# Moving the value products and the turning within the early steps of a fused attention and squared-ReLU kernel

## Chip, core and metric

The kernel runs on one core of a Trainium2 chip. The metric is the device time of one execution in microseconds (us). The profile is one more execution of the same program, recorded by the hardware profiler. Engines are named as in it: PE (TensorE), PEld (its weight loads), DVE (VectorE), ACT (ScalarE), POOL (GpSimd) and SP (SyncE). L387 is line 387 of the kernel before.

## What is computed

Attention with a threshold, followed by two matrix products with a squared ReLU between them, all in fp32:

```
scores = q @ k^T / 8                          # 8 batches x 8 heads, 576 x 576, head size 64
keep   = scores >= max(scores) - tau
w      = where(keep, exp(scores - max(scores)), 0);  w = w / sum(w)
x      = (w @ v), the 8 heads side by side    # 4608 tokens x 512
out    = (max(x @ w_in, 0) ** 2) @ w_out      # 512 -> 2048 -> 512
```

## The kernel before

**Steps.** The attention goes through pairs of heads ("visits"), and through each visit in blocks of 128 query rows, four whole ones and a short one of 64 rows (block 4), in which both heads are put side by side in one operand (`qmid`). One block of one visit is a step. The first eight steps are blocks 0 and 1 of four head pairs, the next twelve blocks 2, 3 and 4 of the same pairs, so that the first 256 tokens of x are complete early; then come whole visits of five steps. Up to step 34 the weights are turned by PE ("turned" means transposed, so that the keys lie on partitions). From step 35 on DVE and DMA turn them, in a different routine.

**What a step does.** Step s works on three blocks at once:

- its own block: scores on PE (L273, L266 for the short block) into PSUM banks 0 to 3, maxima on DVE (L310), three small ACT instructions and the exponentials on ACT (`exponents`, L322, L323, L325), threshold and sum on DVE (L337 to L340), division on POOL (L345, L347, `divide`). The next step's scores of a head write where the threshold of this step reads, so they follow it;
- the block of step s-2: its weights are turned, `turn(vis, i, part)`. Each of three parts is three transposes on PE (L386) into one PSUM bank and a copy on ACT into `wT` (L387). The short block has eight narrow transposes in two parts (L393, L395) and two in the third (L399, L400);
- the block of step s-3: its values, `mix`. Ten matmuls with v (L502, twenty records in the trace) go into one PSUM bank, and ACT copies the result into the token buffer `xT` (`put`, L485).

Values and turning take their banks in turn from 4 and 5 (`take("tx", (4, 5))`). Only in the first ten steps, while `early()` holds, the turning's second part takes from 6 and 7 instead. A matmul into a bank waits until the copy that empties the bank has run.

**Other work in the same steps.** Each step can round one or two pieces of the second stage's weights (`round_weights`, stages 0 to 4): two ACT instructions (L149, L150), two on DVE (L152, L154), two on POOL (L156, L158). The first piece's ACT part is issued at the very start of a step, ahead of the scores, and a second piece's behind the exponentials. Three buffers serve in turn, so a rounding waits for the POOL part of the third last piece. Once 256 tokens of x are complete, `add_chunk` puts the matmuls of the second stage in a list, 16 pieces of `x @ w_in` (L548, followed by ACT's L558 and POOL's square L559) and then pieces with `w_out` (L730). `fill` takes pieces out of the list to put them between the attention's PE work, as `rate` spreads them over the steps to come.

**Order.** The program is issued by hand, in the order of the code; each engine has one queue in that order. In the main loop of a step the lines that matter here are 1106 to 1202: round_weights stage 0, scores and maxima, turning parts 0 and 1 (L1127), exponents (L1131), a second piece's rounding, the qmid copies (`split_left`, L242, in the second step of a visit), the first fill, values with `add_chunk` (L1149), turning part 2 (L1153), threshold and the other rounding stages, the other fills, and last the end of the rounding. `mixes` says at which step which values are made, `chunk_at` at which step a chunk of 256 tokens is complete.

Of the kernel before, what the change touches and what calls it, by code (L numbers as in the profile page):

```python
# [19 lines left out]
def kernel(  # L20
# [177 lines left out]
    def some_loads():  # L198
        for _ in range(min(1 + (len(loads) > 8), len(loads))):
            to, src = loads.popleft()  # L200
            nc.sync.dma_start(out=to, in_=src)
# [117 lines left out]
    def exponents(vis, i):  # L319
        w, sc, st = weights[vis, i]  # L320
        mx, thr, bias = (st[:, j, 0:len(sc)] for j in range(3))
        nc.scalar.activation(out=bias, in_=mx, func=AF.Copy, scale=-SCALE)  # L322
        nc.scalar.activation(out=thr, in_=mx, func=AF.Identity, bias=ntau8)  # L323
        for u in range(len(sc)):
            nc.scalar.activation(out=w[:, u, :].rearrange("p (h k) -> p h k", h=2), in_=sc[u],  # L325
                                 func=AF.Exp, bias=bias[:, u:u + 1], scale=SCALE)
# [27 lines left out]
    def take(what, among):  # L354
        used[what] += 1
        return bank[among[used[what] % len(among)]]
# [21 lines left out]
    def turn(vis, i, part):  # L378

        w = weights[vis, i][0]  # L380
        ps = take("mm", (6, 7)) if early() and part == 1 else take("tx", (4, 5))
        ps = ps.rearrange("p (c n) -> p c n", n=P)
        if i < NBLK:
            for n in range(3):
                c = 3 * part + n
                nc.tensor.transpose(ps[:, n, :], w.rearrange("p u k -> p (u k)")[:, c * P:(c + 1) * P], ident)  # L386
            nc.scalar.copy(wT[:, 2 * i:2 * i + 2, 3 * part:3 * part + 3, :].rearrange("p g c q -> p c g q"),  # L387
                           ps[:, 0:3, :].rearrange("p c (g q) -> p c g q", g=2))
        elif part < 2:
            rows = slice(part * D, (part + 1) * D)  # L390
            for c in range(NBLK):
                at = part * REST + c * P
                nc.tensor.transpose(ps[:, c, 0:D], w[rows, 0, at:at + P], ident[rows, rows])  # L393
            at = part * (NBLK + 1)
            nc.scalar.copy(wT[:, 2 * NBLK, at:at + NBLK, :], ps[:, :, 0:D])  # L395
        else:

            for rows, keys in ((slice(0, D), slice(S - REST, S)), (slice(D, P), slice(0, REST))):
                nc.tensor.matmul(ps[rows, 0, 0:D], w[rows, 0, keys], ident[rows, rows], start=True, stop=True)  # L399
            nc.scalar.copy(wT[:, 2 * NBLK, NBLK, :], ps[:, 0, 0:D])  # L400
# [98 lines left out]
    def mix(n, cols):  # L499

        def term(ps, u, c, at, rows=slice(0, P), first=False, last=False):
            nc.tensor.matmul(ps[u * D:(u + 1) * D, :], vs[n % 2][rows, u * (NBLK + 1) + c, :],  # L502
                             wT[rows, at // REST:(at + ps.shape[1]) // REST, NBLK if c == NBLK else u * (NBLK + 1) + c, :],
                             start=first, stop=last)

        above, below = slice(0, D), slice(D, P)
        arrived(vs[n % 2])
        if not by_dma(n):
            ps = take("tx", (4, 5))[:, 0:cols.stop - cols.start]
            for c in range(NBLK + 1):  # L510
                for u in range(2):
                    term(ps, u, c, cols.start, first=(c == 0), last=(c == NBLK))
            put(n, cols.start, ps, False)
            return
        n1, n2 = 2 * P + REST, 2 * P
        at = ODD if paired(n) and n % 2 else ONE
        one, two = bank[0], bank[4]
        groups = (one[:, 0:n1], at, (above, below)), (two[:, 0:n2], TWO, (below, above))
        for ps, x, _ in groups:
            for c in range(NBLK):  # L520
                for u in range(2):
                    term(ps, u, c, x, first=(c == 0))

        for ps, x, places in groups:
            for u, rows in enumerate(places):
                term(ps, u, NBLK, x, rows, last=True)
        put(n, 0, one[:, ONE - at:ONE - at + 2 * P], True)
        left = ODD if at == ODD else LEFT - at
        put(n, NBLK * P, one[:, left:left + REST], False)
        put(n, 2 * P, two[:, 0:n2], True)  # L530
# [303 lines left out]
    mixes = {}  # L834
# [16 lines left out]
    chunk_at, j = {}, 0  # L851
# [11 lines left out]
    def early():  # L863
        return state["step"] < min(chunk_at)
# [16 lines left out]
    def add_chunk(j):  # L881
        waiting.extend(pieces_of(j))
        whole.add(j)
# [212 lines left out]
    for s in range(END + 1):  # L1096
        state["step"] = s
        if s >= first_late:
            assert 4 not in kept.values()
            late_step(s)  # L1100
            continue
        state["usable"] = rounded_by[-1]
        rounded_by.append(state["rounded"])
        on = s < NST
        now = []
        if on:
            n, i = steps[s]
            at = visits[n][1].index(i)
            last = at == len(visits[n][1]) - 1
            now = list(range(done, done + pieces[s]))  # L1110
            done += pieces[s]
            more = n + 1 < len(visits)
            short = n < 2 * HP
            if short and at == 0 and 0 < n + 1 < 2 * HP:
                load_qk(n + 2)
            elif not short and at == 1 and not by_dma(n):
                load_qk(n + 1)
            if now:
                round_weights(now[0], 0)
            if s != 1:  # L1120
                scores(s)
                after()
                some_later("gpsimd")
        old = steps[s - 2] if 2 <= s < NST + 2 and not by_dma(steps[s - 2][0]) else None
        at_once = now or old or early()
        lay = on and last and more and not by_dma(n) and s != 1
        if old:  # L1127
            turn(*old, 0)
            turn(*old, 1)
        if on:  # L1130
            exponents(n, i)  # L1131
            if s and by_dma(steps[s - 1][0]):
                turn_last(s)
            for p in now[1:]:
                round_weights(p, 0)
            if at == 1:
                split_left(n)
            if lay:
                prep(n + 1)
            elif now:  # L1140
                for p in now:
                    round_weights(p, 1)
        if s in mixes and not old:
            mix(*mixes[s])
            for j in chunk_at.get(s, ()):
                add_chunk(j)
        quarter = rate(s) / 4 if s < END else 1e9
        fill(quarter)
        if s in mixes and old:  # L1149
            mix(*mixes[s])  # L1150
            for j in chunk_at.get(s, ()):
                add_chunk(j)
        if old:  # L1153
            turn(*old, 2)
        state["free"] = s > first_dma
        if s == 0:
            scores(1)
            prep(1)
        smooth = s > first_dma + 2 and s not in mixes
        some_later("vector")  # L1160
        some_later("gpsimd")
        if smooth:
            after()
        if on:
            threshold(n, i)
            for fn in prep_at[s] + load_at[s]:
                fn()
            if lay and now:
                round_weights(now[0], 1)
            if now:  # L1170
                round_weights(now[0], 2)
                round_weights(now[0], 3)
            for p in now[1:]:
                assert not lay
                round_weights(p, 2)
                round_weights(p, 3)
            if not at_once:
                divide(n, i)
        if smooth:
            fill(quarter)  # L1180
            after()
            some_later("gpsimd")
        for what in place_at[s]:
            place_blocks(*what)
        some_loads()
        some_later("vector")
        if not smooth:
            some_later("gpsimd")
            fill(quarter)
        some_loads()  # L1190
        if on and at_once:
            divide(n, i)
        fill(quarter)
        some_loads()
        fill(quarter)
        some_loads()
        if on:
            for p in now:
                end_rounding(p)
            if at == 0 and 0 < n <= 2 * HP:  # L1200
                load_v(n)
            elif last and n >= 2 * HP and not by_dma(n):
                load_v(n + 1)
# [35 lines left out]
```

## Time and profile before

| what | value |
|---|---|
| median of 3 runs | 1334.75 us (1334.66 to 1335.83) |
| the profiled execution's own time | 1334.19 us |
| its span in the profile | 1332.4 us |
| mean granted TensorE clock | 0.995 |
| PE busy | 1297.2 us, 97% of the span |
| PE weight loads busy | 1078.2 us, 81% |
| DVE busy | 928.2 us, 70% |
| POOL busy | 758.3 us, 57% |
| ACT busy | 585.2 us, 44% |
| mean HBM traffic | 133 GB/s |

The busy times are sums over the whole span. Since the engines work on different blocks at the same moment, an engine's share doesn't tell by itself what the end waits for; this is read from the chain of waits (each piece of work that ended last before the next could start) and from the timeline, by stage. The first steps start at 8.50 us (steps 0 and 1), 14.64 (step 2), 21.48 (step 3) and 28.84 (step 4); step 10 starts at 59.68 us, step 20 at 120.43 and step 35 at 210.18.

### The profile page before, as it was taken

What the parts mean: (1) busy time and instruction counts of PE and PEld (TensorE: products, weight loads), DVE (VectorE), ACT (ScalarE), POOL (GpSimd) and SP (SyncE); (2) the same over time, 40 slices, a digit from 0 to 9 for tenths busy, and PEclk for the clock granted to TensorE, in tenths of its full rate; (3) what the DMA queues carried; (4) which work ended last, traced back from release to release, by engine and by line L of the source; (5) the groups of instructions that cost most, each with busy time, mean ns of one, the idle gap of its engine ahead of it and who ended that gap; (6) DMA issues with size and microseconds to landing.
All of it is one profiled execution on the core that took longest, in us unless ns stands there. A gap on an engine that the chain in (4) does not pass through costs nothing.

```text
span 1332.4 us, 25133 instructions
## 1 busy us (share of the span) xinstructions
PE 1297.2 (97%) x9112; PEld 1078.2 (81%) x9112; DVE 928.2 (70%) x2026; ACT 585.2 (44%) x1357; POOL 758.3 (57%) x865
## 2 busy tenths in 40 slices
PE   7898999999999999999999999999999999999998
PEld 5676556878796979787888888888887888889997
DVE  6877776777787878777786777868687877732131
ACT  4776674235262535343434443444434343422321
POOL 4689875765655555364655554737274737354451
PEclk7999999999999999999999999999999999999999
DMA  8764531647767686867586685758677577430000
GB/s 159 160 152 117 144 91 36 160 93 183 167 177 170 169 195 165 200 141 200 123 186 147 172 192 138 189 108 205 138 181 169 150 180 164 141 91 1 17 17 16
DMA packets 330124, 186.68 MB, mean 140 GB/s; under 512 B 291440, under 2 KB 291472, under 8 KB 323600
## 3 DMA queue, kind: packets, MB, share of 16 engines
q1 hardware_dynamic: 317696, 116.87, 45.0%
q10 hardware_dynamic: 9504, 59.27, 11.2%
q0 software_dynamic: 2800, 8.93, 1.8%
q8 instruction: 72, 1.18, 0.4%
q14 instruction: 52, 0.43, 0.1%
HBM read 109.22 MB, written 68.42 MB: 133 GB/s over the span
## 4 chain that ended last, share of the span: by engine, by line
PE 85%; DVE 5%; ACT 4%; DMA 3%; POOL 2%; issue 1%; SPq 1%; ACTq 0%; DVEq 0%; POOLq 0%
PE big L659 28%; PE big L765 27%; PE big L502 10%; PE big L289 8%; PE big L548 3%; PE big L273 3%; PE big L730 2%; PE big L386 2%; DMA wT<-aside 2%; DVE st L310 1%; DVE w L337 1%; ACT w L325 1%; ACT wT L387 1%; DMA aside<-turned 1%; PE big L266 0%
## 5 line engine op out<-in xcount | busy, mean ns | idle before, releaser
L337 DVE SCALAR_TENSOR_TENSOR w<-big,st,w 128x576 f32<-128x576 f32 x269 | 207.2, 807 | 97.8 <-ACT w L325 97.5
L310 DVE TENSOR_REDUCE st<-big 128x1 f32<-128x576 f32 x288 | 204.3, 748 | 86.2 <-PE big L289 53.5
L347 POOL TENSOR_SCALAR w<-w,st 128x576 f32<-128x576 f32 x269 | 247.4, 929 | 28.0 <-DVE st L340 24.0
L765 PE MATMUL big<-wo,gsum 128*128 128x256 f32 x1088 | 243.8, 382 | 0.0
L345 POOL TENSOR_SCALAR st<-st 128x2 f32<-128x2 f32 (+1 forms) x148 | 36.6, 247 | 358.6 <-DVE w L337 354.2
L765 PEld LDWEIGHTS big<-wo,gsum 128*128 128x128 f32 x1088 | 204.4, 190 | 37.1 <-issue 8.6
L659 PE MATMUL big<-xT,w_in_sb 128*128 128x128 f32 x1536 | 187.3, 277 | 0.8 <-DVE g L671 0.7
L659 PEld LDWEIGHTS big<-xT,w_in_sb 128*128 128x128 f32 x1536 | 178.5, 192 | 9.8 <-issue 7.6
L765 PE MATMUL big<-wo,g 128*128 128x256 f32 x816 | 185.3, 382 | 0.1
L325 ACT ACTIVATE w<-big,st 128x576 f32<-128x576 f32 x269 | 183.8, 734 | 0.2 <-ACT st L323 0.2
L502 PE MATMUL big<-wT,vs 128*64 128x128 f32 (+5 forms) x1700 | 164.8, 355 | 9.7 <-ACT wT L387 4.2
L765 PEld LDWEIGHTS big<-wo,g 128*128 128x128 f32 x816 | 151.6, 190 | 26.1 <-issue 6.5
L502 PEld LDWEIGHTS big<-wT,vs 128*64 128x64 f32 (+1 forms) x1700 | 97.3, 137 | 73.9 <-issue 21.5
L322 ACT ACTIVATE st<-st 128x2 f32<-128x2 f32 (+1 forms) x148 | 30.3, 205 | 263.4 <-DVE st L310 262.2
L671 DVE TENSOR_TENSOR g<-big,g 128x512 f32<-128x512 f32 x96 | 64.8, 677 | 82.3 <-PE big L659 76.4
L289 PE MATMUL big<-kT,qT 64*128 64x320 f32 (+3 forms) x768 | 108.0, 416 | 0.2 <-DVE w L337 0.2
L289 PEld LDWEIGHTS big<-kT,qT 64*128 64x128 f32 x768 | 84.5, 186 | 15.7 <-issue 4.3
L538 POOL TENSOR_TENSOR gsum<-g 128x512 f32<-128x512 f32 x34 | 46.1, 1356 | 81.6 <-ACT g L668 72.1
L667 ACT ACTIVATE g<-g 128x512 f32<-128x512 f32 x96 | 60.3, 628 | 61.0 <-DVE g L671 59.4
L668 ACT ACTIVATE g<-g 128x512 f32<-128x512 f32 x128 | 80.7, 630 | 4.1
L431 DVE STREAM_TRANSPOSE turned<-w 128x512 f32<-128x512 f32 x100 | 70.3, 703 | 3.7 <-DMA aside<-turned 2.6
L437 DVE STREAM_TRANSPOSE turned<-w 128x512 f32<-128x512 f32 x100 | 66.9, 669 | 0.0
(113 smaller groups left out, 1973.2 us busy)
## 6 DMA issues: line engine op xcount, KB each, us to landing
aside<-turned ACTq DMA_DIRECT2D x50, 1152.0 KB, 5.2
wT<-aside SPq DMA_DIRECT2D x200, 288.0 KB, 5.5
vs<-in_v_dram SPq DMA_DIRECT2D x72, 128.0 KB, 4.4
ql<-in_q_dram SPq DMA_DIRECT2D x126, 72.0 KB, 2.9
wo<-in_moe_w_in_dram SPq DMA_DIRECT2D x16, 512.0 KB, 4.8
wo<-in_moe_w_out_dram SPq DMA_DIRECT2D x16, 512.0 KB, 3.7
out_dram<-osb POOLq DMA_DIRECT2D x32, 256.0 KB, 3.3
kl<-in_k_dram SPq DMA_DIRECT2D x113, 72.0 KB, 3.0
```

The costliest lines, as they stand in the source:

```text
L289: nc.tensor.matmul(big[to, at + x0:at + x1], lhsT, keys[u * D:(u + 1) * D, x0:x1], start=True, stop=True)
L310: nc.vector.tensor_reduce(out=mx[:, u:u + 1], in_=sc[u], axis=AX.XY, op=ALU.max)
L325: nc.scalar.activation(out=w[:, u, :].rearrange("p (h k) -> p h k", h=2), in_=sc[u], func=AF.Exp, bias=bias[:, u:u + 1], scale=SCALE)
L337: nc.vector.scalar_tensor_tensor(out=wu, in0=sc[u], scalar=thr[:, u:u + 1], in1=wu, op0=ALU.is_ge, op1=ALU.mult, accum_out=sm[:, u:u + 1])
L347: nc.gpsimd.tensor_scalar(out=w[:, u, :], in0=w[:, u, :], scalar1=z[:, u:u + 1], scalar2=rcp[:, u:u + 1], op0=ALU.add, op1=ALU.mult)
L431: move(wb[:, 0:h, :, :], whole_[:, 0, :, :, :])
L437: move(wb[:, h + 1:, :, :], whole_[:, 1, :, :, :])
L502: nc.tensor.matmul(ps[u * D:(u + 1) * D, :], vs[n % 2][rows, u * (NBLK + 1) + c, :], wT[rows, at // REST:(at + ps.shape[1]) // REST, NBLK ...
L659: nc.tensor.matmul(to[:, f, :], factor(j, p, q, c)[:, f * P:(f + 1) * P], part[:, c, :], start=(p in "125" and f == 0 and c == 0), stop=(p ...
L668: nc.scalar.activation(out=to, in_=to, func=AF.Square)
L671: nc.vector.tensor_tensor(out=x, in0=to, in1=x, op=ALU.add)
L765: nc.tensor.matmul(to, left[:, f, :], wo[:, slot, f, :], start=(f == 0), stop=(f == HF - 1))
```

## The change

Only the order of issue in steps 2 to 36 changes; no instruction is added, removed or given another shape. In each step that turns a block,

- the values of the block before are issued right behind the scores, and `add_chunk` with them, so it also runs ahead of `rate` and the first fill;
- the exponentials are issued next, behind the values and their copy, ahead of the turning and of ACT's copies of it;
- turning parts 0 and 1 come behind the exponentials, but ahead of a second rounding piece and of the qmid copies;
- turning part 2 goes to the end of the step, behind the last fill.

```diff
@@ -1125,10 +1125,16 @@
         at_once = now or old or early()
         lay = on and last and more and not by_dma(n) and s != 1
         if old:
+            if s in mixes:
+                mix(*mixes[s])
+                for j in chunk_at.get(s, ()):
+                    add_chunk(j)
+        if on:
+            exponents(n, i)
+        if old:
             turn(*old, 0)
             turn(*old, 1)
         if on:
-            exponents(n, i)
             if s and by_dma(steps[s - 1][0]):
                 turn_last(s)
             for p in now[1:]:
@@ -1146,12 +1152,6 @@
                 add_chunk(j)
         quarter = rate(s) / 4 if s < END else 1e9
         fill(quarter)
-        if s in mixes and old:
-            mix(*mixes[s])
-            for j in chunk_at.get(s, ()):
-                add_chunk(j)
-        if old:
-            turn(*old, 2)
         state["free"] = s > first_dma
         if s == 0:
             scores(1)
@@ -1194,6 +1194,8 @@
         some_loads()
         fill(quarter)
         some_loads()
+        if old:
+            turn(*old, 2)
         if on:
             for p in now:
                 end_rounding(p)
```

## Prediction

> **What bounds the kernel now.** I call one pass of the main loop a step and number it as the code does; it begins where its scores (L273, or L266 for the short block) start. First the windows view, cut where the change ends to act: the three stretches that follow are steps 4 to 9, steps 10 to 35, and most of the rest.
>
> ```profile
> 28.84:59.68 30.84, 26.49 (x223) 19.52 (x223) 24.68 (x60) 22.65 (x58) 17.88 (x24) 1.00 0.79 158
> 59.68:223.81 164.13, 152.49 (x1168) 105.77 (x1168) 118.44 (x262) 113.80 (x280) 130.22 (x141) 1.00 0.46 116
> 223.81:1200.00 976.19, 970.35 (x6798) 818.61 (x6798) 733.66 (x1619) 402.64 (x933) 549.77 (x629) 1.00 0.67 160
> ```
>
> After the stretch come busy times of PE, weight loads, DVE, ACT, POOL. Past 223.81 PE is busy 99% of the time and the change leaves that part's order alone, so what is won or lost before comes out at the end undiminished. Only the first 224 us are open: PE idles 4.4 us in steps 4 to 9 and 11.6 us in steps 10 to 35, where POOL is busy 79%. Next the chain of waits in an early step (7) and in a later one (14):
>
> ```profile
> 43.94 1.97 PE big L273 x7
> 45.91 0.49 PE big L386 x3
> 46.42 0.86 ACT wT L387 x2
> 47.48 0.75 ACT wo L325
> 48.25 0.84 DVE wo L337 x2
> ...
> 82.12 1.17 PE big L273 x8
> 83.29 0.81 PE big L386 x6
> 84.10 1.73 PE big L548 x8
> 85.83 1.24 PE big L502 x20
> 87.07 0.48 PE big L386 x3
> 87.55 1.73 PE big L548 x8
> ```
>
> Step 7 is a ring of 5.19 us: scores, first third of the turning, ScalarE's two copies of it, exponential, threshold, next scores. PE is not its bound. Step 14 is PE alone: 7.16 us with two pieces of the second stage (L548), so 5.43 with one and 3.70 with none. The timeline says why ScalarE is in step 7's ring:
>
> ```profile
> 45.25 1.46 DVE L310 TENSOR_REDUCE st<-big 128x1 f32<-128x576 f32 x2
> 46.42 0.86 ACT L387 COPY wT<-big 128x384 f32<-128x384 f32 x2 [2.23 <-PE big L386]
> 46.64 1.31 PE L502 MATMUL big<-wT,vs 128*64 128x128 f32 x20
> 47.17 0.22 ACT L322 ACTIVATE st<-st 128x2 f32<-128x2 f32 x1
> 48.74 0.27 ACT L485 COPY xT<-big 128x128 f32<-128x128 f32 x1
> ```
>
> The maxima end at 46.71, but L322, which opens the exponentials, waits for the copies until 47.17: 0.46 us. And POOL's hand in step 17:
>
> ```profile
> 101.73 2.66 POOL L158 TENSOR_TENSOR w_in_sb<-turned 128x512 f32<-128x512 f32 x2
> 103.19 0.68 ACT L150 ACTIVATE turned<-wo 128x512 f32<-128x512 uint32 x1 [3.15 <-POOL w_in_sb L158]
> 104.44 0.70 PE L548 MATMUL big<-xT,w_in_sb 128*128 128x256 f32 x2 [0.50 <-POOL w_in_sb L158]
> 104.97 0.23 ACT L322 ACTIVATE st<-st 128x2 f32<-128x2 f32 x1
> ```
>
> ScalarE stands 3.15 us at a rounding (L150) until POOL frees its buffer, and the exponentials queue behind.
>
> [...] Here two banks serve values and turning, and PE waits 0.24 us at L502 for a copy of the turning in steps such as 13 and 25. [...] L152 takes 0.42 us alone, and 1.36 us at 138.79 beside POOL's L158. [...] The trace shows 2.40 us for the values at 25.91 and 1.31 us from 31.05 on.
>
> **The change, early steps.** No instruction is added or removed. On PE the values (1.31) move ahead of the turning; on ScalarE the copy of the values (L485) moves ahead of the exponentials with them, and only the copies of the turning go behind. So in step 7 L322 no longer waits for 0.49 + 0.86 of turning; it waits for 1.31 of values and for L485. PE's scores end at 45.91, values then at 47.22; L485 starts 0.05 later (as in step 29, where values end at 182.53 and it starts at 182.58), and the next instruction starts 0.15 after it (48.74 to 48.89): L322 at about 47.4 in place of 47.17. That is 0.20 a step, as the rest of the ring stays: 5 steps (4 to 8), +1.00. Step 2 has no values, so its exponentials do gain: maxima end 19.03, L322 was at 19.55: -0.47. Step 3 runs on the slow clock, values 2.40, and L322 comes 0.7 later, but PE's own work held its end already: +0.10. Step 9 also copies qmid (L242), which step 10's scores need; it stood right behind the exponentials and now stands behind two copies (0.75): 0.20 + 0.75 = +0.95. Sum +1.58.
>
> **Steps 10 to 36.** In these the maxima (1.42) start only when all scores are there, so values (1.24 on the chain) lie beside them: L322 can start 2.75 us after the step's scores, as before (2.73). What changes is PE. Values used to wait for a copy of the turning to free a bank (0.5 us on the chain where no piece lay between); this goes. The chunk is announced before the first filling, so pieces come earlier: by the two programs' instruction order steps 10 to 13 have 1, 2, 1, 0 pieces (before 0, 1, 2, 1), then 2, 2, 0 repeated (before 2, 1, 1), steps 20 to 27 have 2, 2, 1, 2, 1, 1, 2, 1 (before 2, 1, 2, 1, 2, 1, 1, 2), and the same from 28. A step lasts as long as the longer of PE's sum and the ring. Block changes alter 5.43 and 7.16: narrow values (0.73) save 0.5, the short block's turning (0.5 and 0.26 for 0.80 and 0.48) saves 0.5, its scores 0.2.
> Steps 10 to 13: before 22.37 (59.68 to 82.05). After 5.22 (PE), 7.15 (PE), 5.37 (exponentials, two copies, qmid), 4.25 (threshold behind the transposes of DVE) = 21.99: -0.38.
> Steps 14 to 20: before 46.30 (to 128.35). Step 14 stays 7.15. Step 15 rounds two pieces; its second rounding is issued after the turning, so L149, L152 and the threshold come 0.65 later: exponentials end 4.3 into the step, and 0.65 + 0.58 + 0.5 + 0.82 follow: 6.36 becomes 6.87. Step 16 without a piece gets 4.42 for 5.04, but step 17 gives it back: L485 stands behind L150, which POOL releases 7.6 us after step 16's start, and the second third of the turning needs the bank that L485 empties, with two pieces behind it on PE. 7.6 + 0.6 + 0.3 (L485) + 0.4 (turning) + 3.5 (pieces) + 0.5 = 12.9 for both, before 12.96. Step 18, 6.90 (VectorE's L152 then lies beside no L158: 0.43 for 0.95, which pays for its delay); 19 and 20 like 16 and 17. Sum 7.15 + 6.87 + 12.9 + 6.9 + 12.9 = 46.72: +0.42.
> Steps 21 to 24: before 27.47 (to 155.82). After 6.63 (two pieces, short turning), 7.0 (two roundings; VectorE's L152 beside no L158), 7.13 (two pieces), 5.2 (one piece). The last was 8.51 with two, 1.57 of it PE waiting for copies behind L150 behind POOL; POOL's square (L559) moves out of this stretch's way into an idle 2.6 us. Sum 25.96: -1.51.
> Steps 25 to 29: before 28.84 (to 184.66); after 5.43 + 6.63 + 5.2 + 5.43 + 5.2 = 27.89: -0.95, the removed bank waits.
> Steps 30 to 33 had a piece between turning and values: no change. Step 34: L322 waits for values and L485, +0.32. Step 35: two L736 copies no longer straddle the values, so PE's 1.05 us stall at L548 becomes 0.6: -0.37.
> SP's queue keeps its order; POOL's changes only in five squares. Sum 1.58 - 0.38 + 0.42 - 1.51 - 0.95 + 0.32 - 0.37 = -0.89. The profiled execution took 1334.19 us (span 1332.4 and 1.8 around it), so 1333.3; the median of the runs is 0.56 above it: 1333.8.
>
> **What the trace of before doesn't show.** How long ScalarE's backlog holds L485 in the other steps. Roundings (1.16) begin when the last copy is done and end near 1.6 us into a step, values end near 2.45: from below 0, from above 1.2 us as in step 17, in up to 4 more steps. I take 0. The moment at which the clock rises: from -1.1 (step 3's values at 1.31 for 2.40) to +1.5 (a step more on the slow clock, which lasts 6.84 for 5.19). I take 0.
>
> **Rivals.** Slower: L485 becomes the gate. It holds the exponentials and the second third of the turning together, and any rounding that waits for POOL now holds it. It decides once POOL's L158 ends over 1.8 us into a step's scores. For it: POOL's 79%, and three roundings that waited already (6.3 + 2.6 us). Against: between them ScalarE has 0.8 us to spare. Price: four more steps at 1.2 = +4.8, so 1338.6.
> Faster: POOL's chain starts earlier with step 16's scores, and steps 17 and 20 don't pay back (2 x 1.25)[...]: -0.9 - 2.5 - 1.1 = -4.5, so 1330.3. For it: step 17's wait is 3.15 us of POOL alone; against: between the double roundings of steps 15 and 18 (96.95 to 116.78) POOL idles only 1.4 us of 19.8, so it can't run far ahead.
> That the exponentials don't come ahead at all: for the early steps this is the forecast itself, since L485 stays ahead of them. If L485 cost the early ring only 0.05, the sum would be -1.6: 1333.1, inside the forecast.
>
> **How the numbers follow.** About 0.2% (2.7 us) is what a measurement of this kernel can tell from no change. Forecast, 0.50: 1333.8, alone 1332.1 to 1337.4. Slower rival 0.27, near 1338.6; faster rival 0.23, near 1330.3. The range reaches to both, 1330.3 to 1338.6, and leaves their outer parts out. Faster 0.23, same 0.50, slower 0.27.
>
> **What would show it.** In steps 4 to 8 a ring of 5.4 us, with values and L485 in the chain in place of L386 and L387, and L322 right behind L485. Step 10's scores late, behind L242. In steps 17 and 20 L386 waiting for L485 behind L150. Step 24 some 3 us shorter, steps 21, 23 and 26 over 1 us longer. From 224 us on the same distance to the end. I am wrong if the ring gets shorter than 5.19, if L386 waits for L485 in most steps, or if the part after step 36 changes its length.

## The result and the profile after

| | before | after |
|---|---|---|
| median of 5 runs beside each other | 1335.83 us (1334.66 to 1336.67) | 1341.69 us (1340.59 to 1342.33) |
| profiled execution, its span | 1334.19, 1332.4 us | 1341.71, 1339.9 us |
| granted TensorE clock, profiled execution | 0.995 | 0.991 |
| PE busy | 1297.2 us | 1304.5 us |
| start of scores, steps 4, 10, 21, 25, 36, 38 | 28.84, 59.68, 128.35, 155.82, 223.81, 241.37 | 28.57, 62.68, 131.59, 160.40, 228.14, 246.03 |

The changed kernel takes 1.005 times as long (95%: 1.0038 to 1.0062): slower by 6 us, where 1333.8 us was forecast and 1338.6 us was the end of the range. The windows view of the changed kernel, cut at the same work (steps 4 to 9, steps 10 to 35; after the stretch come PE, weight loads, DVE, ACT, POOL, then the clock):

```profile
28.57:62.68 34.11, 27.70 (x222) 21.45 (x222) 25.97 (x62) 23.14 (x61) 18.61 (x24) 0.95 0.77 163
62.68:228.14 165.46, 156.87 (x1168) 108.44 (x1169) 115.15 (x259) 111.56 (x278) 128.86 (x140) 0.99 0.44 113
```

The first stretch is 34.11 us for 30.84, the second 165.46 for 164.13. PE is busy longer in both (27.70 for 26.49, 156.87 for 152.49), and yet has the same matmuls; the last column but two gives one reason: the clock was 1.00 in both stretches before and is 0.95 and 0.99 now. In each of the two it stood at half for 3.41 us, which by estimate costs 1.7 us at most, half of that time. The first stretch's 1.2 us are within that; the second's 4.4 us are not. A further 2 us of them are, by estimate, five steps in which two groups of transposes take 0.89 us for 0.46 (the experiments on the short block). The chain of waits in steps 7 and 14:

```profile
44.77 1.97 PE big L273 x7
46.75 1.29 PE big L502 x20
48.04 0.02 issue
48.06 0.27 ACT xT L485
48.33 0.10 ACT st L322
...
48.52 0.75 ACT wo L325
...
49.30 0.84 DVE wo L337 x2
...
84.80 1.24 PE big L273 x8
86.04 1.24 PE big L502 x20
87.28 0.94 PE big L386 x6
88.22 3.46 PE big L548 x16
91.68 0.33 PE big L386 x3
```

Step 7 is a ring again, now 5.40 us (5.19 before): values (L502) and their copy (L485) stand where the turning and its copies stood, as the prediction said. Step 14 is PE alone, 7.14 us, as before. The timeline of step 7:

```profile
46.09 1.45 DVE L310 TENSOR_REDUCE st<-big 128x1 f32<-128x576 f32 x2
46.68 1.31 PE L502 MATMUL big<-wT,vs 128*64 128x128 f32 x20
48.06 0.27 ACT L485 COPY xT<-big 128x128 f32<-128x128 f32 x1 [2.44 <-PE big L502]
48.22 0.21 ACT L322 ACTIVATE st<-st 128x2 f32<-128x2 f32 x1
```

The maxima (L310) end at 47.54 and L322 could run. ACT is idle for 2.44 us, but L485 is ahead of it in the queue, and L485 waits until PE has done the values. L322 starts 0.68 us after the maxima; it was 0.46. In step 17 the wait for POOL is still there, shorter, and the second third of the turning waits for L485 behind it, as predicted:

```profile
106.79 0.67 ACT L150 ACTIVATE turned<-wo 128x512 f32<-128x512 uint32 x1 [2.18 <-POOL w_in_sb L158]
107.36 0.25 ACT L485 COPY xT<-big 128x128 f32<-128x128 f32 x1
107.66 0.55 PE L386 MATMUL big<-ident,w 128*128 128x128 f32 x3 [1.11 <-ACT xT L485]
```

What the prediction had not seen is in the windows of PE. The record of the granted clock holds only 1.00 and 0.50 in the profiles of the two kernels. In the changed one half the clock stands from 13.45 to 27.10 us, then three times for 3.41 us, beginning at 57.82, 146.56 and 573.23 us. The view is cut at these edges: three windows, each with the one that follows it (PE busy, then clock, DMA share, GB/s):

```profile
54.40:57.82 3.42, 2.36 (x16) 1.00 0.85 182
57.82:61.23 3.41, 3.41 (x26) 0.50 0.93 264
143.15:146.56 3.41, 1.53 (x8) 1.00 0.18 31
146.56:149.98 3.42, 3.42 (x18) 0.50 0.72 253
569.82:573.23 3.41, 1.28 (x10) 1.00 1.23 182
573.23:576.64 3.41, 3.34 (x16) 0.50 0.51 65
```

Each time a window in which PE is busy for 38 to 69% is followed by one at half the clock. PE's longest single gaps there were 1.06 us ahead of step 9, 1.66 in step 22 and 2.20 at 571 us. The matmuls then take longer: scores 2.98 us for 1.24 in step 23, values 2.12 for 1.31 in step 9 and 4.26 for 2.63 at 573 us. The kernel before has no stretch at half speed between the start, up to 28.5 and 29.1 us in its two profiles, and the end, although PE idles there too:

```profile
148.01:151.42 3.41, 1.84 (x22) 1.00 0.06 11
151.42:154.84 3.42, 3.42 (x21) 1.00 0.81 229
```

So the busy time of a window does not decide alone (1.84 us here without a fall, 2.36 at 54.40 with one); the part on why the prediction was wrong comes back to it. Over the 70 executions of the kernel before in the comparisons below the granted clock is 0.994 to 0.996; over the five of the changed kernel it is 0.989 to 0.994.

### The profile page after: what moved, and what is told of

Its sections match the earlier page's. It is cut to its first block, busy times and chain, and to the rows that moved or that the text cites. A ratio compares the mean times of both kernels' runs of the same rounds, so it can differ in the third digit from the quotient of the medians.

```text
span 1339.9 us, 25103 instructions
## 1 busy us (share of the span) xinstructions
PE 1304.5 (97%) x9112; PEld 1083.1 (81%) x9112; DVE 924.5 (69%) x2026; ACT 582.8 (43%) x1357; POOL 755.8 (56%) x865
## 4 chain that ended last, share of the span: by engine, by line
PE 85%; DVE 5%; DMA 4%; ACT 3%; SPq 1%; POOL 1%; issue 1%; ACTq 0%; DVEq 0%; POOLq 0%
PE big L659 29%; PE big L765 27%; PE big L502 11%; PE big L289 8%; PE big L273 3%; PE big L548 3%; PE big L730 2%; PE big L386 1%; DMA wT<-aside 1%; DVE w L337 1%; DVE st L310 1%; ACT w L325 1%; DMA aside<-turned 1%; DMA vs<-in_v_dram 1%; DVE wo L718 1%
## 5 line engine op out<-in xcount | busy, mean ns | idle before, releaser
L310 DVE TENSOR_REDUCE st<-big 128x1 f32<-128x576 f32 x288 | 204.5, 748 | 90.7 <-PE big L289 54.0
L347 POOL TENSOR_SCALAR w<-w,st 128x576 f32<-128x576 f32 x269 | 247.0, 927 | 28.5 <-DVE st L340 24.2
L502 PE MATMUL big<-wT,vs 128*64 128x128 f32 (+5 forms) x1700 | 167.6, 359 | 4.2 <-DMA wT<-aside 3.3
L502 PEld LDWEIGHTS big<-wT,vs 128*64 128x64 f32 (+1 forms) x1700 | 99.0, 139 | 72.0 <-issue 26.3
L322 ACT ACTIVATE st<-st 128x2 f32<-128x2 f32 (+1 forms) x148 | 30.1, 203 | 263.6 <-DVE st L310 263.1
```

What stands on the lines that cost most here:

```text
L310: nc.vector.tensor_reduce(out=mx[:, u:u + 1], in_=sc[u], axis=AX.XY, op=ALU.max)
L347: nc.gpsimd.tensor_scalar(out=w[:, u, :], in0=w[:, u, :], scalar1=z[:, u:u + 1], scalar2=rcp[:, u:u + 1], op0=ALU.add, op1=ALU.mult)
```

## The experiments

Theory "waits": L485 ahead of the exponentials, and what else the new order makes wait, costs the time. Rival "clock": the waits are small, and the time is lost in half-speed stretches, taken to come from PE's idle time. Step lengths are from one profiled execution each, from the start of one step's scores to the next one's. The start of step 3 moves by up to 1.4 us between executions of one kernel, so sums are also given from there to step 38's scores: 219.89 us before, 225.00 after.

**Exponentials ahead of the values in the early steps.**

```diff
+        if on and early():
+            exponents(n, i)
         if old:
             if s in mixes:
...
-        if on:
+        if on and not early():
             exponents(n, i)
```

> The changed kernel, but in the early steps the exponentials are issued ahead of the values, so that the copy of the values (L485) stands behind them on ScalarE; later steps as in the changed kernel. Theory 'waits' (the early ring is 5.40 us because L485 stands ahead of the exponentials): the ring of steps 4 to 8 falls to about 4.7 us (5.40 less 0.5 for the values and 0.2 for the copy beyond the maxima), seven steps of it give 4 us: about 1337.5 us for 1341.7. Rival 'clock' (the loss is lost TensorE clock after idle gaps, the ring itself costs nothing or little): with PE as the next bound of the ring or with its idle gaps shorter the time moves with the granted clock alone; if the dips at 57.5 and 145.5 us stay, at most 1 us is won.

Measured: 1336.96 us, 1.0008 (0.9999 to 1.0017) of before, so nearly all of the loss is gone. Step 3 to step 38: 220.19 us. But the ring is 5.07 us and not 4.7. The timeline of PE in its step 7 shows L485 once more:

```profile
45.02 0.88 PE L386 MATMUL big<-ident,w 128*128 128x128 f32 x6
46.87 0.55 PE L386 MATMUL big<-ident,w 128*128 128x128 f32 x3 [0.98 <-ACT xT L485]
47.35 0.99 PE L273 MATMUL big<-kT,qT 64*128 64x288 f32 x4
```

L485 now stands behind the exponentials, and the last third of the turning, which uses the bank that L485 empties, waits 0.98 us for it, with the next scores behind. The ring gave 0.33 us a step. About half of the 4.8 us between steps 3 and 38 came from the clock, by estimate from two steps: step 3 left the slow clock of the start earlier (5.90 us for 7.54, 1.6 less), which may be luck, since the next run issues step 3 in the same order and took 7.28; and step 9 stayed on the full one (values 1.31 for 2.12, 0.8 less). So each theory has half of it. The slow stretches at 143 and 569 us stayed.

**The same, and a bank of its own for the last third.**

```diff
-        ps = take("mm", (6, 7)) if early() and part == 1 else take("tx", (4, 5))
+        ps = take("mm", (6, 7)) if early() and part else take("tx", (4, 5))
```

> The run before it (exponentials ahead of the values in the early steps), with the last third of the turning in a bank of its own in the early steps, since there the ring was 5.07 us, with PE waiting 0.84 us for L485, which had gone behind the exponentials, to empty the bank that this third takes. Theory (L485 held that ring too, through the bank): the ring falls to 4.7 us (5.40 less 0.20 for L485 and less 0.49 for a place ahead of the copies), 0.35 less for six steps: step 10 starts 2.1 us sooner than with the exponentials ahead alone. Rival (PE's own sum of some 4.6 us or the threshold holds the ring as well): 5.0 us, under 0.5 us won.

Measured: 1334.95 us, 0.9997 (0.9988 to 1.0006) of before. The ring is 4.67 to 4.88 us in turn, and its timeline shows nothing between turning and scores but the threshold:

```profile
46.39 0.20 ACT L322 ACTIVATE st<-st 128x2 f32<-128x2 f32 x1 [1.79 <-DVE st L310]
46.73 1.20 PE L386 MATMUL big<-ident,w 128*128 128x128 f32 x9
47.93 0.27 ACT L485 COPY xT<-big 128x128 f32<-128x128 f32 x1
48.47 0.75 PE L273 MATMUL big<-kT,qT 64*128 64x288 f32 x2 [0.53 <-DVE wo L337]
```

So L485 held both rings, first through ACT's queue and then through the bank; its rival (PE or the threshold hold the ring at 5.0) falls. The gain of 2.1 us at step 10 did not come in the profiled execution: step 3 took 7.28 us for 5.90, and step 5 had a half-speed stretch (5.89 us), so that step 10 started 0.85 us later than in the run above. The clock takes and gives more than this wait.

**Two thirds of the short block in one bank.**

```diff
-        ps = take("mm", (6, 7)) if early() and part == 1 else take("tx", (4, 5))
-        ps = ps.rearrange("p (c n) -> p c n", n=P)
+        if i < NBLK or part != 1:
+            ps = take("mm", (6, 7)) if early() and part == 1 else take("tx", (4, 5))
+            used["turning"] = ps
+        if i == NBLK:
+            ps = used["turning"][:, part % 2 * 4 * D:(part % 2 + 1) * 4 * D].rearrange("p (c n) -> p c n", n=D)
+        else:
+            ps = ps.rearrange("p (c n) -> p c n", n=P)
```

> The changed kernel, but the two thirds of the short block's turning use two halves of one PSUM bank, so that the second no longer waits for L485 to empty the bank of the values. Theory 'waits': steps 15, 18, 21, 26 and 31 are shorter by 0.36, 0.25, 0.5, 0.5 and 0.5 us, 2.2 in sum: about 1339.5 us. Rival 'clock': TensorE only waits elsewhere (the chain of the threshold holds those steps), under 0.7 us is won: 1341 to 1341.7.

Measured: 1355.5 us, 1.0152 (1.0138 to 1.0166) of before, a miss for both. The steps grew, 15, 18 and 21 to 8.99 us, 26 to 10.58 (with a half-speed stretch in it, one of five in this profile after the start): PE waits 1.82 us for the copy of the first third, which stands behind the exponentials. In step 15 the first four transposes end at 98.48 us, that copy at 100.25, and the second four start at 100.30. The edit put a longer wait for the one it took away, and so did not tell the theories apart.

**Second third of the short block behind half of the pieces; and both thirds there.** The second of these (labelled as the pair) moves part 0 with it.

```diff
             turn(*old, 0)
-            turn(*old, 1)
+            if old[1] < NBLK:
+                turn(*old, 1)
...
         fill(quarter)
+        if old and old[1] == NBLK:
+            turn(*old, 1)
```

> The changed kernel, with the second third of the short block's turning issued behind the first half of the pieces of its step, so that the pieces lie beside PE's wait for L485 to empty the bank. Theory 'waits': steps 15, 18, 21, 26 and 31 fall from 7.23, 7.15, 7.16, 7.16 and 5.44 us to 6.87, 6.9, 6.63, 6.63 and 4.9: 2 us sooner by step 36. Rival (L485 stands behind other work than this shows, or the sum of PE was taken too small): these steps stay within 0.15 us of what they were.

> The changed kernel, with both thirds of the short block's turning (one on array rows 0 to 63, one on 64 to 127) issued together behind the first half of the pieces. In the kernel before the 8 took 0.46 us together; in the changed one the second four wait for L485, so that the two groups run one behind the other, 0.86 us, and the run that set them apart on purpose kept those 0.86 us. Theory (the wait for L485 costs the pair's running side by side): steps 15, 18, 21, 26 and 31 fall by 0.4 us each from 7.23, 7.15, 7.16, 7.16 and 5.44: 2 us by step 36. Rival (the pair is not what holds these steps): under 0.1 us a step.

Measured with the second third alone moved (one run, 1343.27 us): steps 15, 18, 21, 26 and 31 take 7.31, 7.30, 7.30, 7.15 and 5.39 us, within 0.15 us of what they were, as its rival said. With both moved (one run, 1340.69 us): 7.09, 6.93, 6.93, 7.15 and 5.53, so 0.14, 0.22 and 0.22 less in three of the five. The two total times say little, for both runs have one more half-speed stretch in the early ring (at 42.8 us, step 6: 6.31 and 6.26 us for 5.40), and the first a doubled one at 148.6 us (step 23: 10.67). What PE does in step 15 of the kernel before, in step 15 of the changed one, and in step 21 of the one with the pair, in this order:

```profile
90.28 0.46 PE L393 MATMUL big<-ident,wo 64*128 64x64 f32 x8
```

```profile
94.35 0.89 PE L393 MATMUL big<-ident,wo 64*128 64x64 f32 x8
95.17 3.72 PE L548 MATMUL big<-xT,w_in_sb 128*128 128x256 f32 x16
```

```profile
136.15 1.99 PE L548 MATMUL big<-xT,w_in_sb 128*128 128x256 f32 x8
138.07 0.48 PE L393 MATMUL big<-ident,wo 64*128 64x64 f32 x8
138.48 1.99 PE L548 MATMUL big<-xT,w_in_sb 128*128 128x256 f32 x8
```

Before, the eight took 0.46 us, and the records of the two groups overlap (90.28 to 90.74). After, four alone take 0.46 (94.35 to 94.81); the second four wait for L485's bank and start at 94.78, 0.89 in all. Moved together they take 0.48 again, but a run of pieces that is cut in two costs 0.2 us (3.84 from start to start over both pieces, 3.65 for the 16 in one go), which eats half of it. In step 26 the filling stood behind the pair, and nothing changed. So the theory is right on the place and half right on the size: L485 costs the pair 0.4 us a step; this edit can't give all of it back.

**Second rounding and qmid ahead of the turning.**

```diff
-        if old:
-            turn(*old, 0)
-            turn(*old, 1)
         if on:
             if s and by_dma(steps[s - 1][0]):
                 turn_last(s)
             for p in now[1:]:
                 round_weights(p, 0)
             if at == 1:
                 split_left(n)
+        if old:
+            turn(*old, 0)
+            turn(*old, 1)
+        if on:
             if lay:
```

> The changed kernel, but the second rounding of a step with two (L149, L150) and the copies of qmid (L242) stand ahead of the turning again, behind the exponentials. Theory 'waits': step 10's scores no longer wait for two copies (0.75 us), and steps 15, 18 and 22 have their threshold 0.3 to 0.5 us earlier: 2 us in sum, about 1339.7 us. Rival 'clock': PE's idle time in step 9 falls as well and the dip at 57.5 us goes with it: 0.8 more, about 1339; if these copies are hidden, 1341.7 as before.

Measured: 1338.03 us, 1.0021 (1.0014 to 1.0028) of before. Step 9 falls from 7.10 to 5.55 us, step 22 from 7.00 to 6.53, 15 and 18 stay (7.15). Of step 9's 1.55 us, 0.75 are the copies ahead of qmid, as priced, and 0.8 the clock, which stayed at 1.00 there. From step 4 to 57 us this kernel does what the changed one does, with the same rings of 5.40 us and the same idle 1.06 us ahead of step 9's scores. A window with this gap has PE busy as long as the changed kernel's (2.35 us for 2.36), and no slow stretch follows:

```profile
52.60:56.01 3.41, 2.35 (x23) 1.00 0.70 109
56.01:59.43 3.42, 3.42 (x35) 1.00 0.92 231
```

So this idle time alone doesn't bring it; what else does was not shown. At 145 us, where PE's idle time stayed, the slow stretch stayed (step 23: 9.30 us).

**Small matmuls in PE's idle time.**

```diff
+    def fill_idle(to, times):
+        for x in range(times):
+            nc.tensor.matmul(to[:, x % 4 * P:x % 4 * P + P], ident, ident, start=True, stop=True)
...
+        if s == 22:
+            fill_idle(bank[(4, 5)[used["tx"] % 2]], 3)
         if old:
             turn(*old, 2)
+        if 4 <= s <= 9:
+            fill_idle(bank[(6, 7)[(used["mm"] + 1) % 2]], 8 if s == 9 else 3)
+        elif s == 22:
+            fill_idle(bank[(4, 5)[(used["tx"] + 1) % 2]], 5)
```

> The changed kernel with small matmuls added where PE idles (3 at the end of steps 4 to 8, 8 at the end of step 9, 3 and 5 around the last third of the turning in step 22; their results are used by nothing). Theory 'clock': the dips of the granted clock at 57.5 and 145.5 us come from PE's idle gaps before them; filled, they go: 2.5 to 3 us are won, about 1339 us, and every run's granted clock is at 0.994 or above. Theory 'waits', or dips that come at random: the same time as the changed kernel, 1341.7, or up to 1 us more for the added matmuls, with dips as before.

Measured: 1339.74 us, 1.0034 (1.0022 to 1.0047) of before. The windows of PE in the changed kernel, then in this one:

```profile
57.00:63.00 6.00, 4.86 (x33) 0.72 0.67 187
145.00:156.00 11.00, 10.25 (x49) 0.84 0.30 98
```

```profile
57.00:63.00 6.00, 5.84 (x56) 1.00 0.60 171
145.00:156.00 11.00, 11.00 (x78) 1.00 0.35 105
```

More work on PE, and less time: step 3 to step 38 takes 222.07 us for 225.00. Both dips are gone. Step 9 takes 6.30 us for 7.10. Step 23 takes 7.28 for 9.38, but step 22 grew from 7.00 to 7.48 by the added matmuls, so the two together give 1.6 us, near the 1.7 us estimated for 3.41 us at half speed. The other 0.5 us are step 3's, which stands ahead of every added matmul (7.04 for 7.54). Not every clock came to 0.994: the five executions have 0.992 to 0.995, and this profile has a half-speed stretch of its own at 271 us, in a part that the edit leaves alone. The median is 2 us lower, but its interval overlaps with the changed kernel's (1.0038 to 1.0062), so the gain is read from the steps and not from the total.

**Chunk announced behind the first filling, as before.**

```diff
             if s in mixes:
                 mix(*mixes[s])
-                for j in chunk_at.get(s, ()):
-                    add_chunk(j)
...
         fill(quarter)
+        if s in mixes and old:
+            for j in chunk_at.get(s, ()):
+                add_chunk(j)
```

> The changed kernel, with the pieces of a new chunk announced behind the first filling of a step, as in the kernel before, so that the pieces fall to the steps as there (2, 1, 1 for 2, 2, 0). Theory (the slow clock at 145.5 us comes from the step ahead of it, which has two roundings and only one piece, so that PE idles 2.7 of 7 us): step 22 has two pieces, step 23 falls from 9.38 us to about 6, and step 24 goes back to 8.5 of before or less: steps 21 to 24 27 to 27.5 us for 28.8. Rival (slow clocks come at random, not from the filling of steps): the sum of steps 21 to 24 stays 28.8 or a dip appears elsewhere.

Measured: one run, 1336.79 us. Steps 21 to 24 take 5.43, 8.16, 5.30 and 7.32 us: 26.21 for 28.81, and 27.47 in the kernel before. No slow stretch at 145 us; PE now has two pieces in step 22, where two roundings meet, and fewer in the steps that are full anyway. Step 3 to step 38: 222.33 us, 2.7 less than the changed kernel. The rival's sign came as well: a half-speed stretch at 121.3 us (step 19: 6.27 us), behind 1.99 us of idle PE, where the changed kernel has none. The mended kernel at the end has the same order of pieces and no such stretch (step 19: 4.84 us). The slow clock of step 23 was there in every kernel that kept one piece and unfilled idle time in step 22 (steps 23 of 9.19 to 10.67 us, six kernels beside the changed one), and in none of the four that changed this.

**The exponentials alone moved ahead, in the kernel before.**

```diff
+        if on:
+            exponents(n, i)
         if old:
             turn(*old, 0)
             turn(*old, 1)
         if on:
-            exponents(n, i)
```

> One part of the change alone, on the kernel before: the exponentials are issued ahead of the first two thirds of the turning, the values stay behind them. The prediction's reason for the early ring (0.46 us of it is L322 behind the copies of the turning; L485 is not in it as the values stay behind): steps 4 to 8 fall from 5.19 to about 4.75 us, step 10 starts 2.5 to 3 us sooner than before. Rival (values and last third now wait for copies behind the exponentials): 5.1 us or more, no gain; in steps 10 to 35 PE then waits for L387 behind the exponentials at L502, up to 1 us a step: slower by 5 us or more in all.

Measured: 1379.11 us, 1.0341 (1.0326 to 1.0355) of before; the early ring is 5.28 us, no gain. The rival was right, and its 5 us far too low. In PE's groups from 60 to 260 us, then the timeline of step 15:

```profile
L502 PE MATMUL big<-wT,vs 128*64 128x128 f32 (+1 forms) x500 | 33.8, 287 | 45.6 <-ACT wT L387 30.5 <-ACT wT L395 15.1
```

```profile
98.46 0.47 PE L393 MATMUL big<-ident,wo 64*128 64x64 f32 x8
102.08 1.31 PE L502 MATMUL big<-wT,vs 128*64 128x128 f32 x20 [3.15 <-ACT wT L395]
```

PE stands 45.6 us at the values (5.8 us in the kernel before, from 60 to 220 us), for the bank of a third of the turning whose copy has gone behind maxima and exponentials. In step 15 nothing behind it in PE's queue starts for 3.15 us. Six half-speed stretches between 69 and 217 us add to it (granted clock 0.93 from 63 to 140 us, 0.89 to 156, 0.92 to 224). What holds the early ring at 5.28 us was not looked into. So the two halves of the change belong together: the exponentials may go ahead of the copies only if the values go ahead of the turning.

**The kernel before once more** (one more profile of it, no edit).

> The kernel before once more, for a second profile of it. If the 0.9 to 3.6 us that the changed kernel and its variants lose between 540 and 600 us belong to the change, none is lost here; if they come with the transfers of a run by chance, this profile can show such a loss too, and its start of scores 2 and 3 may differ from the first profile by up to 1.4 us as those of the variants do.

Measured: 1334.95 us. The first steps, up to step 3's scores, took 14.31 us for 12.97, so that step 3 started 1.43 us later, and from step 3 to 38 it is 220.06 us for 219.89: the part that the change touches repeats to 0.2 us, the start on the slow clock doesn't. Between 540 and 600 us it loses nothing: values there wait 1.03 us for a transfer, 1.36 in the first profile. In the changed kernel and in the one with the added matmuls:

```profile
573.30 4.26 PE L502 MATMUL big<-wT,vs 128*64 128x256 f32 x24 [2.20 <-DMA wT<-aside]
```

```profile
573.21 2.63 PE L507 MATMUL big<-wT,vs 128*64 128x256 f32 x24 [2.25 <-DMA wT<-aside]
```

The same wait, and the values take 4.26 us once and 2.63 the other time. Of ten changed orders (waits of 1.39 to 2.25 us) two show the slow stretch (values 4.26 and 4.27 us, 2.63 in the other eight). Why the transfer is waited for longer than in the kernel before was not settled.

**Mends together.** First the exponentials ahead with the bank for the last third, second rounding and qmid ahead of the turning, the short block's second third behind half of the pieces, and the added matmuls in step 22 only; then the same without any added matmul, with the chunk behind the first filling and the short block's pair together.

The second one's edit (the first has only part 1 of the short block behind the filling, and `add_chunk` as in the changed kernel):

```diff
-        ps = take("mm", (6, 7)) if early() and part == 1 else take("tx", (4, 5))
+        ps = take("mm", (6, 7)) if early() and part else take("tx", (4, 5))
...
+        if on and early():
+            exponents(n, i)
         if old:
             if s in mixes:
                 mix(*mixes[s])
-                for j in chunk_at.get(s, ()):
-                    add_chunk(j)
-        if on:
+        if on and not early():
             exponents(n, i)
-        if old:
-            turn(*old, 0)
-            turn(*old, 1)
...
                 split_left(n)
+        if old:
+            if old[1] < NBLK:
+                turn(*old, 0)
+                turn(*old, 1)
+        if on:
...
         fill(quarter)
+        if s in mixes and old:
+            for j in chunk_at.get(s, ()):
+                add_chunk(j)
+        if old and old[1] == NBLK:
+            turn(*old, 0)
+            turn(*old, 1)
```

> All mends together: exponentials ahead of the values and a bank of its own for the last third in the early steps, second rounding and qmid ahead of the turning, the short block's second third behind half of the pieces, and small unused matmuls around the last third in step 22. Theory 'waits and clock', the sum of what each gave at step 38 against the changed kernel: 4.7 for the exponentials, 2.1 for the bank, 0.8 of e3's 2.4 that lies outside step 9, 2 for the short turning, 1.6 for step 22: 11 us, against 4.65 lost, so about 6 us ahead of the kernel before at step 38 and 1329 to 1331 us. Rival (the mends overlap, one wait takes another's place): 2 us ahead of before, 1333 to 1334.

> Mends together without any added matmul: exponentials ahead of the values and a bank of its own for the last third in the early steps, second rounding and qmid ahead of the turning, the chunk announced behind the first filling as before, the short block's two thirds together behind it. Theory, from what each gave at step 38 against the changed kernel: 3.9 to 4.7 for the exponentials and the bank, 0.8 for e3 outside step 9, 2.7 for the chunk, up to 2 for the pair: 9.4 to 10.2, so 5 us ahead of before at step 38: 1329 to 1331. Rival (the slow clock comes back in another step, as PE still idles where two roundings meet): 1333 to 1335.

Measured: 1332.35 us, 0.9985 (0.9974 to 0.9996) of before, and 1331.11 us, 0.9976 (0.9967 to 0.9985) of before. At step 38 they are 2.60 and 5.12 us ahead of the kernel before. In the first, step 22 grew to 8.59 us (7.00 after), where the added matmuls waited 1.70 us for a copy of the turning and then took 2 us themselves, so its sum fell short, nearer to the rival's. The second came out as summed up, at step 38; 0.6 of its 5.12 us are the start of step 3, which moves by itself, and 1.4 step 3, the last on the slow clock of the start. Over ten executions the median is 2.8 us below the kernel before's, and the interval stays below 1. Its PE in steps 22 and 23:

```profile
133.08 1.89 PE L548 MATMUL big<-xT,w_in_sb 128*128 128x256 f32 x8
134.81 1.02 PE L730 MATMUL big<-wo,g 128*128 128x512 f32 x2
137.20 1.13 PE L730 MATMUL big<-wo,g 128*128 128x512 f32 x2 [1.37 <-ACT g L558]
138.16 0.49 PE L386 MATMUL big<-ident,w 128*128 128x128 f32 x3
138.58 1.24 PE L273 MATMUL big<-kT,qT 64*128 64x288 f32 x8
139.75 1.31 PE L502 MATMUL big<-wT,vs 128*64 128x128 f32 x20
```

PE still idles 1.37 us, but two pieces are in the step, the clock stays up, and scores and values take their 1.24 and 1.31. This order beats both kernels by a little.

## Why the prediction was wrong, term by term

| term (step of the sum) | predicted | measured |
|---|---|---|
| early steps, to the start of step 10 | +1.58 | +3.00 |
| steps 10 to 13 | -0.38 | -0.25 |
| steps 14 to 20 | +0.42 | +0.49 |
| steps 21 to 24 | -1.51 | +1.34 |
| steps 25 to 29 | -0.95 | -0.35 |
| steps 30 to 33 | 0 | +0.19 |
| step 34, step 35 | +0.32, -0.37 | +0.33, -0.42 |
| step 36 | 0 | +0.33 |
| from 234 us to the end | 0 | +2.86 |
| sum | -0.89 | +7.52 |

Measured are the differences of the two profiled executions, whose times are 1341.71 and 1334.19 us.

**Right.** The mechanism of the early ring and its size (5.40 us for 5.19, predicted 0.20 a step), L485 and not the turning ahead of L322, qmid late in step 9, L386 behind L485 behind L150 in steps 17 and 20, the longer steps 34 and the shorter 35, and the order of pieces. Steps 10 to 20 are met to 0.2 us, as a sum.

**The step that failed: "The moment at which the clock rises ... I take 0".** The clock stood in the prediction only as the start of the run, with -1.1 to +1.5 us. With the changed order PE also fell back to half the clock in the middle of the run. Three stretches did it, by estimate from the lengths of steps and values: 0.8 us in step 9 (7.10 us, where 5.35 of before and the 0.95 of the prediction make 6.30, which is what the kernels with the filled idle time and with the late chunk took), 1.6 us in steps 22 and 23 (16.39 us together, 14.76 with the idle time filled), 1.6 us at 573 us (4.26 for 2.63): 4.0 of the 7.5. For step 23 this is shown from two sides, by filling the idle time (9.38 us became 7.28) and by moving a piece into it (5.30). For step 9 it is not: four of six kernels with the 5.40-us ring had the fall. Without clock the table's early steps are +2.2, steps 21 to 24 -0.3.

**What goes with the falls, as far as the traces show.** The two profiled executions of the table, cut into 3.413 us each from the end of the start's slow stretch to 1310 us, give 747 windows at full clock. PE was busy for 1.28, 1.53 and 2.36 us in the three that half the clock followed. Six others were busy for less than 2.36 us (1.84 to 2.31), so busy time does not part them. A count of the columns that PE streams does: 0.83 ns each (L273 records of 288 columns start 0.24 us apart at 28.84 us in the kernel before), weighted with the rows times columns that the record names, as a share of 128 x 128. The three have 1,328, 763 and 1,480 columns (at 569.82, 143.15 and 54.40 us), all others 1,814 or more; the window of the kernel before shown above has 1,908.

By this count no 3.41 us of the kernel before, wherever they begin after step 4's start, have fewer than 1,664 columns. In the changed kernel they can have 1,424 in the early ring and 763 in steps 22 and 23. The count was found afterwards, on three falls, and tested on no new run: that it decides is not shown.

**Terms that were sized wrongly.** Step 4: +0.69 for +0.20, for in the kernel before this step was not the full ring yet (4.70 us, not 5.19; 5.06 in its second profile), and afterwards it is (5.40). Short block's turning: "saves 0.5" took the 0.46 us of two groups side by side; apart they take 0.89, and steps 15, 18, 21 and 26 came out at 7.23, 7.15, 7.15 and 7.15 for 6.87, 6.90, 6.63 and 6.63, together 1.7 us (in the sum of steps 14 to 20 that is hidden, as steps 16, 17, 19 and 20 came out 0.5 shorter than predicted). This is the slower rival's place, L485 ahead of a part of the turning, but not its price (1.2 us a step) and not its reason (POOL). That it is the whole of these 1.7 us is not shown: the edit that put the pair together gave back 0.6 us. Late part: "leaves that part's order alone" is true, and its waits still changed: 1.6 us are the dip, the other 1.2 longer waits for transfers, which differ between executions too: from step 38 on the profiles without a half-speed stretch there take 1090.1 to 1092.0 us, the kernel before 1091.0 and 1090.1, the changed one 1092.2 without its dip.

**The rivals and the signs.** The slower one named L485. Undoing its place in the early steps alone brought the time back to within 0.1% of before's, half of it through the clock, so it had the right instruction. The price was paid in clock at least as much as in waits. Of the three signs of being wrong only one came, the part after step 36, 2.86 us longer; the ring did not get shorter, and L386 was seen waiting for L485 in steps 17 and 20 alone. The faster one (POOL ahead, slow start shorter) has nothing for it in steps 17 and 20, 8.33 and 8.32 us. The range ended at 1338.6 since no half-speed stretch was in any case.

## What to carry to other kernels

Price PE's idle time twice: as time, and as a risk that the clock drops (here for 3.41 us at a time); look at the windows view, in windows as long as the shortest stretch at half speed, for those in which an order leaves PE busy for about two thirds or less, and try small pieces there ahead of full steps (steps 21 to 24: 26.21 us for 28.81). Few of them fell: in the two profiles of the table half the clock followed 3 of the 12 windows with PE busy for less than 69.5%, and none of the other 735. When an instruction is moved ahead in an engine's queue, ask what it waits for there (L485 waited for the values, ACT idle for 2.44 us in step 7) and who waits for it through a buffer (0.98 us with the exponentials ahead) as well as through the queue. Two moves can be worth nothing or a loss each and still a gain together, so test them apart before the sum is believed.

## What the runs showed of the hardware that was not expected

- The clock dropped without a long gap: windows of 3.41 us with PE busy 2.36, 1.53 and 1.28 us were followed by one at half the clock, the longest single gap in them 1.06, 1.66 and 2.13 us. With waits of 1.97 to 2.25 us at about 570 us it happened in two of five kernels, so the length of the wait alone did not tell.
- The three stretches at half speed of the changed kernel last 3.41 us each and begin 88.75 and 426.67 us apart, 26.0 and 125.0 times that length. What one costs is estimated at 1.7 us at most, half its length; the values at 573 us took 4.26 us for 2.63.
- In the two profiles of the table the weighted columns that PE streams in 3.413 us part the three falls from the rest (up to 1,480; 1,814 or more in the other 744 windows), where busy time doesn't.
- The short block's transposes on rows 0 to 63 and on rows 64 to 127 took 0.46 us, all eight, with overlapping records, and 0.89 when the second four started 0.43 us after the first.
- In one run matmuls that nothing uses went with less time: with 8 of them steps 22 and 23 took 14.76 us for 16.39, and the granted clock from 145 to 156 us was 1.00 for 0.84. Step 9 lost its fall too (0.8 us), with 23 of them in steps 4 to 9, but two kernels without them had none there either.
